# Attention output packed into 128 rows before the output projection, with a larger exponential ring and a new tile table

## The chip, the core and the metric

The kernel runs on one core of a Trainium2 chip. Its time is device microseconds of one execution. The engines are PE (TensorE, the matmuls), ACT (ScalarE), DVE (VectorE), POOL (GpSimd) and SP (SyncE, which here only issues DMAs).

## What is computed

One layer with attention and a feed-forward part side by side, on x of 2048 rows and 512 columns in bf16. There are 32 query heads of 16 columns; all share one key head and one value head.

```python
xn = layernorm(x)                                   # 2048 x 512
q  = (xn @ wq), 32 heads of 16;  k = xn @ wk;  v = xn @ wv     # k, v: 2048 x 16
o  = softmax(q @ k.T / 4) @ v                       # per head, over all 2048 keys
A  = concat(o) @ wo                                 # 2048 x 512
Bf = gelu(xn @ w1 + b1) @ w2 + b2                   # hidden width 1792
out = x + A + Bf
```

## The kernel before

**Stages.** A prologue loads x and the weights, normalises, transposes xn into xnT and makes keys, values and the first queries. Then the attention runs over 4 blocks (tb) of 512 query rows. A block has 8 groups (g) of 4 heads; group number gg = 8 tb + g counts 32 of them. A group has 64 score tiles, one for each head j of the group and each of 16 key tiles; a tile is 128 keys by 512 queries, one PSUM bank. All 2048 tiles are taken three at a time in 683 visits (u). PSUM has two sets of three banks for scores, so visit u+2 can be computed once visit u has been read.

**A visit.** `scores` (matmuls at L845, in four row tiles of 32) fills the three banks. `exp` (L864, ACT) makes the exponentials of two or three of them into the ring E of 20 slots. Where the string DTAB has a digit for the visit, the tile of that number goes to DVE instead: `p1` (L881) turns the score into an int16 that is read as bf16, and `close_batch` (L896) makes four more versions for up to three such tiles at a time; the five are summed with scaled copies of V. A dot in DTAB leaves all three tiles to ACT. `pv_mm` (L885) multiplies with V on PE in four column tiles of 32, one for each head of the group: one matmul for an ACT tile, five for a DVE tile. The result stands in PSUM bank 6 (pO), a head in each 32 rows: 16 rows of output, one row with the softmax sum.

**A group's end.** `o_evac` copies pO to Of (L909, DVE), an SP DMA collects the four rows of sums into den, DVE takes the reciprocal (L913), a DMA writes it to DRAM, four DMAs read it back spread over 32 rows each (rbc), and DVE multiplies Of by rbc into oT (L920). oT is a ring of 10 slots (NOT), each 128 x 512 with head j in rows 32j to 32j+15. The last group of all has its own short way (`o_norm_last`, L923 to L949), through PE transposes rather than DMAs.

**The out projection.** The weights wop are laid out like oT: 128 rows for each group, of which 4 x 16 hold rows of wo, the others zeros, and b2 in one of the rows that oT fills with ones. For each of 16 row tiles of 128, `out_tile` runs 14 steps of the feed-forward's second matmul (`y_mm`) and 8 steps on oT and wop (`wo_mm`), all into bank 7 (pM), each step as four column-tile matmuls by the helper `mm4` (L560). DVE adds x (L1010) and SP stores. Out tiles of block tb run in the beginning of block tb+1. For the last block, `y_tile` does the 14 steps and groups 0 to FIN_G - 1 ahead of time, the remaining groups follow at the end (L1133 on), and group 31 last.

**What sets the order.** The class `Prog` collects every operation with its reads, writes and an estimated duration, then `schedule` plays them through a model of the engines and fixes for each engine (and SP's DMAs) one order; `emit` writes these orders out with the semaphore waits that the dependences need. An argument `after` only shapes this order and makes no wait. A DMA counts in the model as 0.7 us of SP and 2.2 us to landing. Each DMA has a semaphore of its own stream; what waits for DMAs of several streams gets a wait instruction for each. Side work on PE (column-tile matmuls that are not pv) has a due time, ready time plus an allowance such as Y_ALLOW, and scores go first. Where PE would fall idle, the order gets fillers on zeros (L1152).

Of the kernel before, what the change touches and what calls it, by code (L numbers as in the profile page):

```python
# [10 lines left out]
P = 128  # L11
# [24 lines left out]
EV_ALLOW = -2.0  # L36
S_WAIT = 0.1
P_WAIT = 0.0
NE_ND_KB = (20, 8, 3)
LA = 34  # L40
LB = 105
LY = 9
LP = 121
LS = 107
FIN_G = 4
FIN_F = 0
LAL = 30.0
LCO = 0.0
PRO_FROM = 2.0
TBL = 1  # L50
DTAB = "....2.2020.202.2.2...22.202222..2022.20...2..2..20220.0.2222....2020.20.0202.0.002...2022.200...2.2000.0..220.2.2.0.202002020....002.2.22.0.2002.2...2.222002..02220.02...202.222202.02.2222....022222.202022..222...22200.00.0222.2022...2.20..22.2.2.20.20.....2020..2.22002020....20.22..020.222....0..22.0..2222.0...0220...20.00.0220.2200.22...22222.02.220.22220...2.22020.202202.022....2020.000.2200.2.0....202.2.2..220.0..2.0...0....2.0.2...22.00.....02220.2.222020.0....2.220.20...222222...2.22022.0022.2.2200....2222.22.202..2.22...2.220202.202.2202.0..2220.0000.222.220.....20.22.2200020..02....2..0...22...2.020.0....020202....2.02.20...2022.22.220.02022....22200222.2.2..202.0..."
Y_ALLOW = 8.0
H_ALLOW = 5.0
YT_ALLOW = (3,3,3,3)
WF_ALLOW = 1.5
# [370 lines left out]
def bass_parallel_sum__grouped_kv_mqa__dense_activation_gelu__prompt_kernel(  # L426
# [15 lines left out]
    S, D = xf.shape  # L442
    F = B_w1.shape[1]
    assert (S, D, F) == (2048, 512, 1792)
    H, Dh = 32, 16
# [3 lines left out]
    TBW = 512  # L449
    NTB = S // TBW  # L450
    HG = 4
    NGR = H // HG
    NE, ND, KB = NE_ND_KB
    NOT = 10
    NV = 1 + len(SPL_K)
    KZ = SPL_K.index(0)
    GAM = 128.0 / LN2 * 0.25
    bf, f32 = dt.bfloat16, dt.float32
    i16, i32 = dt.int16, dt.int32

    with ExitStack() as es:
        def sb(shape, dtype, name):
            return es.enter_context(nc.sbuf_tensor(name, shape, dtype))
# [6 lines left out]
        wvk = sb([P, DT, 2 * Dh], bf, "wvk")  # L470
        wkp = sb([P, DT, 4, 32], bf, "wkp")
        wqp = sb([P, DT, H, 32], bf, "wqp")
        wop = sb([P, NGR, D], bf, "wop")
        w1_sb = sb([P, DT, F], bf, "w1_sb")
        w2_sb = sb([P, FT, D], bf, "w2_sb")
        b1row = sb([FT, P], bf, "b1row")
# [3 lines left out]
        ones = sb([P, P], bf, "ones")  # L480
# [41 lines left out]
        rbc = sb([P, 2, TBW], f32, "rbc")  # L522
        rd_dram = nc.dram_tensor("rden_rows", [NTB * NGR, HG * TBW], f32).ap()
        oT = sb([P, NOT, TBW], bf, "oT")

        pAll = es.enter_context(nc.psum_tensor("pAll", [P, 8 * 512], f32))

        def bank(b, n=1):
            return pAll[:, b * 512:(b + n) * 512]
# [6 lines left out]
        def B(b):  # L536
            return ("bank", b)
# [19 lines left out]
        def mm4(o, l, rh, start, stop, r=(), w=(), allow=1.5, **ak):  # L557
            for j in range(4):
                c = slice(32 * j, 32 * j + 32)
                add("pe", lambda e, c=c, j=j: e.matmul(o[c, :], l[:, c], rh, start=start, stop=stop,  # L560
                                                       tile_position=(0, 32 * j)),
                    r, [(k, j) for k in w] + [k for k in w if k != B(7)], occ=0.216, lat=0.23, allow=allow, kind="side", tag=(None, j), **ak)
# [3 lines left out]
        def dma(eng, o, i, stream, r=(), w=(), lat=2.2, allow=1.0, **kw):  # L566
            return add(eng, lambda e: e.dma_start(o, i), r, w, dma=stream, occ=0.7, lat=lat, allow=allow, **kw)  # L567

        x_view = xf.rearrange("(t p) d -> p t d", p=P)
        for i in range(8):  # L570
            dma("sp", x_sb[:, 2 * i:2 * i + 2, :], x_view[:, 2 * i:2 * i + 2, :], f"d_x{i}",
                w=[("x", 2 * i), ("x", 2 * i + 1)], lat=2.3 + 0.5 * i, due=0.0)
# [8 lines left out]
        def setup(fn, r=(), w=(), occ=0.25, due=0.0, **kw):  # L581
            return add("pool", fn, r, w, occ=occ, lat=0.15, due=due, **kw)
# [17 lines left out]
              r=["wk_s", "wkp"], w=["wkp"], occ=0.45, due=2.0)  # L600
# [6 lines left out]
              r=["mrow"], w=["isc"], due=10.0)  # L607
        setup(lambda e: e.memset(crow[0:1, :], 1.13 * GAM * GAM), w=["crow"], due=10.0)
        setup(lambda e: e.memset(V1[:, :, :, Dh:32], 0.0), w=["V1"], occ=1.4, due=11.0)
        for v, c in enumerate((1.0,) + SPL_C):  # L610
# [3 lines left out]
              r=["mask4", "sel8"], w=["sel8"], due=12.0)  # L614
# [155 lines left out]
        for _, _, kind, a in sorted(steps, key=lambda s: s[:2]):  # L770
# [14 lines left out]
            r=[("std", LN_B[-1][0])] + ([("KT", ti) for ti in range(NT)] if TBL else []), w=["dum"], n=1600, due=1.0)  # L785
        dve(lambda e: e.tensor_reduce(kmx[:], kmax[:], AX.X, ALU.max), r=[("kmax", 0), ("kmax", NVA)], w=["kmx"], n=40, due=0.0)
        add("pe", lambda e: e.transpose(bank(3)[0:1, 0:P], kmx[:], ident_f[:]), r=["kmx", "ident_f"], w=[B(3)], occ=0.12, lat=0.22,
            due=0.0)
# [3 lines left out]
            r=["mrow"], w=[B(3), "ibi"], n=40, due=0.0)  # L792
        q_first_m(0, 7)
        dve(lambda e: e.tensor_copy(R2[:], bank(3)[:, 256:257]), w=[B(3), "R2"], n=40)
        for va, vb_ in ((0, NVA), (NVA, NT)):
# [3 lines left out]
                due=22.0)  # L799
            dve(lambda e, va=va, vb_=vb_: e.tensor_copy(V1[:, 0, va:vb_, 0:Dh], Vf[:, va:vb_, :]), r=["V1", ("Vf", va)], w=[("V", 0, va)],  # L800
                n=(vb_ - va) * Dh, due=22.1)
        for v, c in enumerate(SPL_C):
            setup(lambda e, v=v, c=c: e.tensor_scalar(V1[:, 1 + v, :, 0:Dh], Vf[:], c, None, ALU.mult),  # L803
                  r=["V1", ("Vf", 0), ("Vf", NVA)], w=[("V", 1 + v, 0), ("V", 1 + v, NVA)], occ=0.45, due=20.0)

        setup(lambda e: e.tensor_copy(wqp[:, :, 4:H, 0:Dh], wq_s[:, :, 64:D].rearrange("p k (h n) -> p k h n", n=Dh)),  # L806
              r=[("u", i) for i in range(8, 12)] + ["wqp"], w=["wqp"], occ=2.7, due=19.0, after=[pr.writer["ibi"]])
        setup(lambda e: e.tensor_scalar(sel8R[:], sel8[:], R2[:, 0:1], None, ALU.mult),
              r=["sel8", "R2"], w=["sel8R"], occ=0.5, due=22.0)
        late = [pr.writer["ibi"]]  # L810
        setup(lambda e: e.memset(wop[:], 0.0), w=["wop"], occ=3.0, due=24.0, after=late)
        setup(lambda e: e.tensor_copy(selL[:], ident[:, 16:113:32]), r=["ident"], w=["selL"], due=24.0, after=late)
        for j in range(HG):
            dma("sp", wop[32 * j:32 * j + Dh, :, :],
                bass.AP(A_wo.tensor, A_wo.offset + j * Dh * D, [[D, Dh], [HG * Dh * D, NGR], [1, D]]),
                f"d_wo{j}", w=["wop"])
        dma("sp", wop[16:17, 0, :], B_b2.rearrange("(o n) -> o n", o=1), "d_b2", w=["wop"])

        TPG = HG * NT
        NTILE = NTB * NGR * TPG  # L820
# [84 lines left out]
        onorm = {}  # L905

        def o_evac(gg):
            i = gg % 2
            dve(lambda e: e.tensor_copy(Of[:, i, :], pO), w=["O", ("Of", i)], allow=0.0)  # L909
            row = Of[16:17, i, :]  # L910
            dma("sp", den[:, i, :], bass.AP(row.tensor, row.offset, [[32 * row.ap[0][0], HG], [1, TBW]]),
                f"d_den{i}", r=[("Of", i)], w=[("den", i)])
            dve(lambda e: e.reciprocal(den[:, i, :], den[:, i, :]), r=[("den", i)], w=[("den", i)], n=120)  # L913
            dma("sp", rd_dram[gg:gg + 1, :], den[:, i, :], f"d_rd{i}", r=[("den", i)], w=[("rd", i)])
            for j in range(HG):
                src = rd_dram[gg:gg + 1, j * TBW:(j + 1) * TBW]
                dma("sp", rbc[32 * j:32 * j + 32, i, :], bass.AP(src.tensor, src.offset, [[0, 32], [1, TBW]]),
                    f"d_rb{i}{j}", r=[("rd", i)], w=[("rbc", i, j)])
            tb, g = divmod(gg, NGR)
            onorm[gg] = dve(lambda e: e.tensor_tensor(oT[:, gg % NOT, :], Of[:, i, :], rbc[:, i, :], ALU.mult),  # L920
                            r=[("Of", i)] + [("rbc", i, j) for j in range(HG)], w=[("oT", gg % NOT)], allow=3.0)

        def o_norm_last(gg):  # L923
            tb, g = divmod(gg, NGR)
# [68 lines left out]
                mm4(bank(bk), ub[:, ft, i * P:(i + 1) * P], w2_sb[:, ft, :], start and ft == fts[0], stop and ft == fts[-1],  # L993
                   r=[("u", ft), "w2"], w=[B(bk)], allow=al)

        def wo_mm(tb, i, gs, start=False, stop=True, bk=7, al=1.5):
            for n, g in enumerate(gs):
                assert tb * NGR + g in onorm
                mm4(bank(bk), oT[:, (tb * NGR + g) % NOT, i * P:(i + 1) * P], wop[:, g, :], start and n == 0,
                   stop and n == len(gs) - 1, r=[("oT", (tb * NGR + g) % NOT), "wop"], w=[B(bk)], allow=al)  # L1000

        def store(tb, i):
            ti = tb * 4 + i
# [1 line left out]

        def out_tile(tb, i):
            y_mm(tb, i, al=Y_ALLOW)
            wo_mm(tb, i, range(NGR), al=Y_ALLOW)
            ti = tb * 4 + i
            dve(lambda e: e.tensor_tensor(x_sb[:, ti, :], pM, x_sb[:, ti, :], ALU.add), w=[("x", ti)] + M4, allow=EV_ALLOW)  # L1010
            store(tb, i)
# [3 lines left out]
        def y_tile(tb, i):  # L1015
            ti = tb * 4 + i
            y_mm(tb, i, al=YT_ALLOW[i])
            wo_mm(tb, i, range(FIN_G), stop=i < 3, al=YT_ALLOW[i])
            if i < 3:
                dve(lambda e: e.tensor_tensor(xpy[:, i, :], pM, x_sb[:, ti, :], ALU.add), r=[("x", ti)],  # L1020
                    w=M4 + [("x", 2 * i), ("x", 2 * i + 1)], allow=EV_ALLOW)
            else:
                mm4(pM, ident, x_sb[:, ti, :], False, False, r=["ident", ("x", ti)], w=[B(7)], allow=YT_ALLOW[i])
# [57 lines left out]
        par, cgn = [0, 0], [0] * HG  # L1081
        if DTAB:
            for u, c in enumerate(DTAB):
                if c != ".":
# [21 lines left out]
        for u in range(NU):  # L1106
# [4 lines left out]
            for t in ts:  # L1111
                gg, kt, j = tile_of(t)
# [18 lines left out]
        tb = NTB - 1  # L1131
        FB = (2, 3, 4, 7)
        for i in range(4):  # L1133
            wo_mm(tb, i, range(FIN_G, NGR - 1), start=i < 3, stop=False, bk=FB[i], al=WF_ALLOW)
        for i in range(4):
            mm4(bank(FB[i]), oT[:, (NTB * NGR - 1) % NOT, i * P:(i + 1) * P], wop[:, NGR - 1, :], False, True,
               r=[("oT", (NTB * NGR - 1) % NOT) if i < 2 else ("oTl", 1), "wop"], w=[B(FB[i])], due=0.0)
        for i in (0, 1, 3, 2):
            ti = tb * 4 + i
            w = [(B(FB[i]), j) for j in range(4)] + ([B(FB[i])] if i < 3 else []) + [("x", ti)]  # L1140
            if i < 3:
                dve(lambda e, i=i, ti=ti: e.tensor_tensor(x_sb[:, ti, :], bank(FB[i]), xpy[:, i, :], ALU.add),
                    r=[("x", 2 * i), ("x", 2 * i + 1)], w=w)
# [7 lines left out]
        if FILL_GAP:  # L1151
            pr.filler = lambda e, j, o: e.matmul((pO if o else pM)[32 * j:32 * j + 32, :], zeros[:, 0:32], xnT[:, 0, 0:TBW],  # L1152
                                                 start=not o, stop=not o, skip_group_check=True,
# [37 lines left out]
```

## Time and profile before

| | |
|---|---|
| Median of 3 runs | 811.87 us (810.36 to 814.0) |
| The profiled execution | 811.03 us, span in the profile 809.2 us |
| Granted TensorE clock, mean | 0.987 |
| Busy: PE, ACT, DVE, POOL | 782.9, 785.3, 739.7, 23.7 us |
| First exponential starts, last one ends | 30.3 us, 799.5 us |
| Exponentials (L864) | 683, busy 748.2 us |
| Out-projection matmuls (wop with oT) | 512, in four bursts from 236.8 us on |
| DMA issues on SP | 301, 130.9 us |

Times in the profile are microseconds unless ns is written. A group line gives line, engine, operation, tiles as out<-in with their shapes, the count, then busy time and mean ns of one, then the idle time of the engine just before them and what ended it. "PEld" is the weight load of a matmul. The chain of waits goes back from the last instruction to what released it, step by step. In the view by stages, each engine has its busy time and the number of its instructions in the stretch, then the granted clock, the DMA share and GB/s.

### The profile page before, as it was taken

The page shows a single profiled execution, that of the slowest core. Times are in us where ns is not written, and L with a number is a line of the kernel's source. Part 1 is how long each engine was busy: PE and PEld are TensorE (multiplying, and loading weights), DVE is VectorE, ACT ScalarE, POOL GpSimd, SP SyncE. Part 2 cuts the span into 40 slices and gives each one's busy share as a digit, 9 for nine tenths or more (in the row PEclk, how much of TensorE's full clock was granted, in tenths as well). Part 3 has the DMA queues.
Part 4 walks back from the last instruction along what each step waited for, and adds up shares of the span by engine and source line. Part 5 has one row for each costly group of instructions (what it writes and reads, how often), then busy time and mean ns, then how long its engine had stood idle before and what let it go on. Part 6 is the DMA issues. An engine that isn't in the chain of part 4 may idle for free.

```text
span 809.2 us, 21055 instructions
## 1 busy us (share of the span) xinstructions
PE 782.9 (97%) x9082; PEld 245.4 (30%) x9082; DVE 739.7 (91%) x1403; ACT 785.3 (97%) x734; POOL 23.7 (3%) x79
## 2 busy tenths in 40 slices
PE   6799999999999999999999999999999999999998
PEld 4322322222323333333232333223232232233223
DVE  7499999999999978999999978799998897999985
ACT  4899999999999999999999999999999999999995
POOL 6500000000000000000000000000000000000000
PEclk7799999999999999999999999999999999999999
DMA  9000000000000000000000000000000000000001
GB/s 307 15 23 15 17 15 15 2 16 15 15 15 22 22 22 10 15 16 15 16 3 22 22 21 22 15 10 8 16 15 16 22 22 22 9 15 16 9 9 41
DMA packets 23975, 19.08 MB, mean 24 GB/s; under 512 B 12369, under 2 KB 19402, under 8 KB 23882
## 3 DMA queue, kind: packets, MB, share of 16 engines
q1 hardware_dynamic: 22298, 17.17, 7.5%
q8 instruction: 72, 1.18, 0.6%
q10 hardware_dynamic: 1584, 0.56, 0.3%
q14 instruction: 21, 0.17, 0.1%
HBM read 14.98 MB, written 2.35 MB: 21 GB/s over the span
## 4 chain that ended last, share of the span: by engine, by line
ACT 81%; PE 17%; DMA 1%; POOL 1%; issue 0%; DVE 0%; ACTq 0%; POOLq 0%
ACT E L864 77%; PE pAll L885 7%; PE pAll L845 5%; PE pAll L560 4%; ACT ub L987 3%; DMA ub<-in_A_wq_dram 1%; PE pAll L554 1%; ACT ub L684 0%; ACT xnT L702 0%; POOL V L803 0%; PE pAll L697 0%; POOL wqp L806 0%; ACT KT L716 0%; PE pAll L1152 0%; ACTq L567 0%
## 5 line engine op out<-in xcount | busy, mean ns | idle before, releaser
L864 ACT ACTIVATE E<-pAll 128x1024 bf16<-128x1024 f32 (+1 forms) x683 | 748.2, 1358 | 2.7 <-PE pAll L845 2.3
L885 PE MATMUL pAll<-Dt,V 128*32 128x512 bf16 x2070 | 362.7, 383 | 0.3 <-DVE Dt L896 0.2
L881 DVE TENSOR_SCALAR Dt<-pAll 128x512 int16<-128x512 f32 x414 | 278.4, 683 | 33.9 <-PE pAll L845 33.0
L885 PE MATMUL pAll<-E,V 128*32 128x512 bf16 x1634 | 297.1, 389 | 1.1 <-DVE Of L909 0.9
L896 DVE TENSOR_SCALAR Dt<-Dt 128x1536 int16<-128x1536 int16 (+2 forms) x584 | 283.1, 529 | 1.0
L845 PE MATMUL pAll<-QT,KT 32*128 32x512 bf16 x2048 | 268.5, 386 | 11.6 <-ACT E L864 4.2
L845 PEld LDWEIGHTS pAll<-QT,KT 32*128 32x128 bf16 x2048 | 67.8, 91 | 289.8 <-ACT E L864 246.5
L885 PEld LDWEIGHTS pAll<-Dt,V 128*32 128x32 bf16 x2070 | 99.1, 94 | 103.3 <-issue 50.8
L560 PE MATMUL pAll<-w_sb,ub 128*32 128x512 bf16 x896 | 115.3, 382 | 0.0
L560 PE MATMUL pAll<-xnT,w_sb 128*32 128x512 bf16 x896 | 109.5, 382 | 0.2
L885 PEld LDWEIGHTS pAll<-E,V 128*32 128x32 bf16 x1634 | 70.3, 93 | 80.8 <-issue 64.8
L560 PE MATMUL pAll<-wop,oT 128*32 128x512 bf16 x512 | 87.8, 381 | 0.0
L973 DVE TENSOR_SCALAR hb<-pAll,b1T 128x512 bf16<-128x512 f32 x56 | 41.6, 742 | 1.7 <-PE pAll L560 1.5
L560 PE MATMUL pAll<-xnT,wqp 128*32 128x512 bf16 x496 | 39.6, 391 | 0.8 <-DVE QT L739 0.4
L560 PEld LDWEIGHTS pAll<-xnT,w_sb 128*32 128x32 bf16 x896 | 29.5, 95 | 21.1 <-issue 7.5
L560 PEld LDWEIGHTS pAll<-w_sb,ub 128*32 128x32 bf16 x896 | 30.8, 95 | 13.2 <-issue 5.9
L987 ACT ACTIVATE ub<-ub 128x1536 bf16<-128x1536 bf16 (+1 forms) x20 | 32.3, 1617 | 0.0
L739 DVE CAST QT<-pAll 128x512 bf16<-128x512 f32 x32 | 21.9, 684 | 10.8 <-PE pAll L560 9.3
L1152 PE MATMUL pAll<-xnT,zeros 128*32 128x512 bf16 x300 | 31.0, 383 | 0.0
L560 PEld LDWEIGHTS pAll<-wop,oT 128*32 128x32 bf16 x512 | 24.5, 95 | 6.7 <-issue 1.5
L909 DVE COPY Of<-pAll 128x512 f32<-128x512 f32 x31 | 21.2, 682 | 0.5 <-PE pAll L885 0.2
L920 DVE TENSOR_TENSOR oT<-Of,rbc 128x512 bf16<-128x512 f32 x31 | 21.1, 682 | 0.0
(113 smaller groups left out, 262.4 us busy)
## 6 DMA issues: line engine op xcount, KB each, us to landing
rbc<-rden_rows SPq DMA_DIRECT2D x124, 64.0 KB, 2.0
w_sb<-in_B_w_dram SPq DMA_DIRECT2D x2, 1792.0 KB, 12.9
x_sb<-in_A_x_dram SPq DMA_DIRECT2D x8, 256.0 KB, 6.6
out_dram<-x_sb SPq DMA_DIRECT2D x16, 128.0 KB, 1.7
QT<-mT SPq DMA_DIRECT2D x60, 2.0 KB
ub<-in_A_wq_dram ACTq DMA_DIRECT2D x1, 512.0 KB, 7.4
wop<-in_A_wo_dram SPq DMA_DIRECT2D x4, 128.0 KB, 2.8
den<-Of SPq DMA_DIRECT2D x31, 8.0 KB
```

Of the source, the lines that this page charges most:

```text
L560: add("pe", lambda e, c=c, j=j: e.matmul(o[c, :], l[:, c], rh, start=start, stop=stop, tile_position=(0, 32 * j)), r, [(k, j) for k in w] ...
L739: dve(lambda e: e.tensor_copy(QT[:, hq, :], bank(bk)), w=[B(bk)] + [(B(bk), j) for j in range(4)] + [("QT", hq)] + [("QTm", hq, j) for j i ...
L845: ins = e.matmul(o, l, rh, start=True, stop=True, tile_position=(q0, 0))
L864: exps.append(act(lambda e: e.activation(E[:, s0:s0 + na, :], bank(b0, na).rearrange("p (a n) -> p a n", a=na), ACT.Exp, scale=LN2 / 128.0 ...
L881: dve(lambda e: e.tensor_scalar(Dt[:, KZ, s, :], bank(bk), float(127 * 128) + SPL_D, SPL_MIN, ALU.add, ALU.max), w=[B(bk), ("D", s, KZ)], ...
L885: add("pe", lambda e, a, b: e.matmul(pO[32 * j:32 * j + 32, :], V1[:, v, kt, :], rhs, start=a, stop=b, tile_position=(0, 32 * j)), r=r + [ ...
L896: dve(lambda e, k=k: e.tensor_scalar(Dt[:, k, s0:s0 + n, :], Dt[:, KZ, s0:s0 + n, :], float(SPL_K[k]), None, ALU.add), r=[("D", s0 + i, KZ ...
L909: dve(lambda e: e.tensor_copy(Of[:, i, :], pO), w=["O", ("Of", i)], allow=0.0)
L920: onorm[gg] = dve(lambda e: e.tensor_tensor(oT[:, gg % NOT, :], Of[:, i, :], rbc[:, i, :], ALU.mult), r=[("Of", i)] + [("rbc", i, j) for j ...
L973: dve(lambda e: e.tensor_scalar(hb[:, ft % 6, :], pM, b1T[:, ft:ft + 1], None, ALU.add), r=["b1T"], w=M4 + [("h", ft % 6)], allow=ev)
L987: act(lambda e: e.activation(uu, uu, ACT.Tanh, scale=GELU_K), r=uk, w=uk, n=c, allow=al - 0.5, kind="tanh")
L1152: pr.filler = lambda e, j, o: e.matmul((pO if o else pM)[32 * j:32 * j + 32, :], zeros[:, 0:32], xnT[:, 0, 0:TBW], start=not o, stop=not o ...
```

## The change

- **Packing.** When a group's oT is done, four DMAs on SP (one for each head, 16 rows of 1 KB) copy its 4 x 16 useful rows into a new ring oTp of 5 slots; an even group fills rows 0 to 63, the odd one after it rows 64 to 127. A slot thus holds 8 heads in 128 rows. oT keeps 3 slots.
- **Weights.** wop becomes wo as it is, 4 tiles of 128 rows, loaded in one DMA with no memset before it. The last group keeps the old layout with weights of its own, wol (a memset and four DMAs). b2 stands in the first row of b2row, the rest zeros.
- **Out projection.** `wo_mm` takes pairs of groups: 4 steps of all 128 rows in place of 8, and `b2_mm` adds a step with ones and b2row. In the last block, `y_tile` takes pairs 0 and 1 and the bias, the end takes pairs 2 and 3 (of pair 3 only group 30; a POOL memset clears the other half of its slot), and group 31 comes last with wol.
- **Ring and table.** E gets 24 slots in place of 20. DTAB is replaced: 416 digits in place of 414, and 212 of 683 entries differ.

```diff
-NE_ND_KB = (20, 8, 3)
+NE_ND_KB = (24, 8, 3)
...
-FIN_G = 4
+FIN_G = 2
...
-DTAB = "....2.2020.202.2.2...
+DTAB = "....2..020..02..22...
...
-    NOT = 10
+    NOT, NPR = 3, 5
...
-        wop = sb([P, NGR, D], bf, "wop")
+        wop = sb([P, NGR // 2, D], bf, "wop")
+        wol = sb([P, D], bf, "wol")
+        b2row = sb([P, D], bf, "b2row")
...
+        oTp = sb([P, NPR, TBW], bf, "oTp")
...
-        setup(lambda e: e.memset(wop[:], 0.0), w=["wop"], occ=3.0, due=24.0, after=late)
+        setup(lambda e: e.memset(wol[:], 0.0), w=["wol"], occ=0.4, due=24.0, after=late)
...
+        dma("sp", wop[:], A_wo.rearrange("(g p) n -> p g n", p=P), "d_wo", w=["wop"], after=late)
         for j in range(HG):
-            dma("sp", wop[32 * j:32 * j + Dh, :, :],
-                bass.AP(A_wo.tensor, A_wo.offset + j * Dh * D, [[D, Dh], [HG * Dh * D, NGR], [1, D]]),
-                f"d_wo{j}", w=["wop"])
-        dma("sp", wop[16:17, 0, :], B_b2.rearrange("(o n) -> o n", o=1), "d_b2", w=["wop"])
+            dma("sp", wol[32 * j:32 * j + Dh, :], A_wo[(H - HG + j) * Dh:(H - HG + j + 1) * Dh, :], f"d_wl{j}", w=["wol"])
+        setup(lambda e: e.memset(b2row[:], 0.0), w=["b2row"], occ=0.4, due=24.0, after=late)
+        dma("sp", b2row[0:1, :], B_b2.rearrange("(o n) -> o n", o=1), "d_b2", w=["b2row"])
...
+            pp, h = divmod(gg, 2)
+            if gg == NTB * NGR - 2:
+                setup(lambda e: e.memset(oTp[64:P, pp % NPR, :], 0.0), w=[("oTp", pp % NPR, 1, j) for j in range(HG)], occ=0.4)
+            for j in range(HG):
+                r0 = 64 * h + Dh * j
+                dma("sp", oTp[r0:r0 + Dh, pp % NPR, :], oT[32 * j:32 * j + Dh, gg % NOT, :], f"d_op{gg % NOT}{j}",
+                    r=[("oT", gg % NOT)], w=[("oTp", pp % NPR, h, j)])
...
-        def wo_mm(tb, i, gs, start=False, stop=True, bk=7, al=1.5):
-            for n, g in enumerate(gs):
-                assert tb * NGR + g in onorm
-                mm4(bank(bk), oT[:, (tb * NGR + g) % NOT, i * P:(i + 1) * P], wop[:, g, :], start and n == 0,
-                   stop and n == len(gs) - 1, r=[("oT", (tb * NGR + g) % NOT), "wop"], w=[B(bk)], allow=al)
+        def wo_mm(tb, i, ps, start=False, bk=7, al=1.5):
+            for n, p in enumerate(ps):
+                pp = tb * NGR // 2 + p
+                hs = [h for h in range(2) if 2 * pp + h < NTB * NGR - 1]
+                assert all(2 * pp + h in onorm for h in hs)
+                mm4(bank(bk), oTp[:, pp % NPR, i * P:(i + 1) * P], wop[:, p, :], start and n == 0, False,
+                   r=[("oTp", pp % NPR, h, j) for h in range(2) for j in range(HG)] + ["wop"], w=[B(bk)], allow=al)
+
+        def b2_mm(bk=7, stop=True, al=1.5):
+            mm4(bank(bk), ones, b2row[:], False, stop, r=["ones", "b2row"], w=[B(bk)], allow=al)
...
-            wo_mm(tb, i, range(NGR), al=Y_ALLOW)
+            wo_mm(tb, i, range(NGR // 2), al=Y_ALLOW)
+            b2_mm(al=Y_ALLOW)
...
-            wo_mm(tb, i, range(FIN_G), stop=i < 3, al=YT_ALLOW[i])
+            wo_mm(tb, i, range(FIN_G), al=YT_ALLOW[i])
+            b2_mm(stop=i < 3, al=YT_ALLOW[i])
...
-            wo_mm(tb, i, range(FIN_G, NGR - 1), start=i < 3, stop=False, bk=FB[i], al=WF_ALLOW)
+            wo_mm(tb, i, range(FIN_G, NGR // 2), start=i < 3, bk=FB[i], al=WF_ALLOW)
...
-            mm4(bank(FB[i]), oT[:, (NTB * NGR - 1) % NOT, i * P:(i + 1) * P], wop[:, NGR - 1, :], False, True,
-               r=[("oT", (NTB * NGR - 1) % NOT) if i < 2 else ("oTl", 1), "wop"], w=[B(FB[i])], due=0.0)
+            mm4(bank(FB[i]), oT[:, (NTB * NGR - 1) % NOT, i * P:(i + 1) * P], wol[:, :], False, True,
+               r=[("oT", (NTB * NGR - 1) % NOT) if i < 2 else ("oTl", 1), "wol"], w=[B(FB[i])], due=0.0)
```

More of the change, by code (lines that the diff above doesn't have):

```diff
@@ L50 @@
 TBL = 1
-DTAB = "....2.2020.202.2.2...22.202222..2022.20...2..2..20220.0.2222....2020.20.0202.0.002...2022.200...2.2000.0..220.2.2.0.202002020....002.2.22.0.2002.2...2.222002..02220.02...202.222202.02.2222....022222.202022..222...22200.00.0222.2022...2.20..22.2.2.20.20.....2020..2.22002020....20.22..020.222....0..22.0..2222.0...0220...20.00.0220.2200.22...22222.02.220.22220...2.22020.202202.022....2020.000.2200.2.0....202.2.2..220.0..2.0...0....2.0.2...22.00.....02220.2.222020.0....2.220.20...222222...2.22022.0022.2.2200....2222.22.202..2.22...2.220202.202.2202.0..2220.0000.222.220.....20.22.2200020..02....2..0...22...2.020.0....020202....2.02.20...2022.22.220.02022....22200222.2.2..202.0..."
+DTAB = "....2..020..02..22...22.202220..20.00.0...220...222200..02200...2.02.2200.00220.02...20222.20...022.0000...2002.0.2.20000.000...2020.2220.0..20020....02.222.0022020..2...202.202202.02.222.....02.222.2022.000.22...20220.00.0222.2022...2220.02..2.2.0022......022...20.202002.2......02.0.000222.00.0..22.0..222..200000......2200.02202.000.22....2220.02.220.22220...22.2020.202202.022....2022.20022.0000.0....20222.220020....220..22..0...0.0..20.00.....022.20..20222.002....20220.20...22022.....0.20202.0.222.220....2220222.00222.2.22...222.0022.00222.0.20...2.020000.222.222.......202.0200.0...02......0...022...22.200....002.202...02.02.20...2022.22..20.020222...22202200..220.2000...."
 Y_ALLOW = 8.0
```

## The prediction

> **What bounds the kernel now.** I read first the page's busy shares and its chain, then the groups with shapes kept apart, then busy time by stage, the waits of PE and ACT, and the timeline of the last 10 us.
>
> ```profile
> PE 782.9 (97%) x9082; PEld 245.4 (30%) x9082; DVE 739.7 (91%) x1403; ACT 785.3 (97%) x734; POOL 23.7 (3%) x79
> ACT 81%; PE 17%; DMA 1%; POOL 1%; issue 0%; DVE 0%; ACTq 0%; POOLq 0%
> L864 ACT ACTIVATE E<-pAll 128x1024 bf16<-128x1024 f32 x415 | 428.1, 1194 | 0.9 <-PE pAll L845 0.8
> L864 ACT ACTIVATE E<-pAll 128x1536 bf16<-128x1536 f32 x268 | 401.0, 1613 | 1.8 <-PE pAll L845 1.5
> ```
>
> Three engines look full, but the chain that ends last is ACT for 81% of the span: the exponentials (L864), one per visit of three score tiles. A visit with one tile sent to DVE (a digit in DTAB) covers two banks, the others three. ACT is idle before them for 2.7 us in all. PE's 97% says less: four column tiles overlap, so a matmul record of 380 ns stands for about 55 ns of issue, and 300 of its matmuls are fillers (L1152, on zeros).
>
> Next, busy time in seven stages from the first exponential to the last, and the out-projection's own matmuls in the same stages:
>
> ```profile
> core 0: us, PE busy (x) PEld busy (x) DVE busy (x) ACT busy (x) POOL busy (x), PEclk, DMA share, GB/s
> 30.30:223.00 192.70, 186.94 (x2045) 54.80 (x2042) 182.82 (x347) 192.38 (x177) 7.78 (x6) 0.98 0.06 15
> 223.00:304.00 81.00, 80.50 (x1026) 24.60 (x1023) 72.49 (x137) 80.77 (x78) 0.00 (x0) 1.00 0.08 20
> 304.00:415.00 111.00, 108.41 (x1179) 33.33 (x1175) 108.78 (x205) 110.03 (x101) 0.00 (x0) 1.00 0.05 13
> ...
> 223.00:304.00 81.00, 24.18 (x128) 7.10 (x128) 0.00 (x0) 1.00 0.08 20
> 799.50:809.20 9.70, 5.14 (x73) 1.82 (x67) 0.00 (x0) 1.00 0.17 56
> ```
>
> The last two rows are for the matmuls on wop alone. Where the out tiles run (223 to 304, and again at 415 and 609) PE is the tight second engine (12.7 matmuls per us) and DVE has air (72.5 of 81); where they don't, DVE is nearly full (108.8 of 111). ACT is full in both.
>
> How much is ACT losing? Starts of successive exponentials, read singly off the timeline, are 0.904 us apart after two banks and 1.331 after three in over half of the visits. DTAB has 414 digits and 269 dots: 414 x 0.904 + 269 x 1.331 = 732.3; 16 long tanh at 1.36 and 4 short at 0.94 (the chain's steps for L987) add 25.5; together 757.8. From the first exponential (30.34) to the end of the last (799.54) are 769.2, so about 11 us of late scores are spread over 683 visits. They, the 9.7 us tail and ACT's own count are all that a change behind the softmax can reach.
>
> **What the skill says.** "ScalarE: Activation LUTs", What ACT_TABLE_LOAD costs, gives one element per cycle, 0.833 ns: 427 ns for 512 columns. The trace agrees: 1.331 - 0.904 = 0.427. "TensorEngine Tiling (Array Packing)", Key Properties, says that changing the tiling mode drains the TensorE; the trace agrees as far as it shows the 0.23 us that the weight load after a score visit loses to "issue" over and over. So time saved inside a visit's column work is real, but no visit goes away. "DMA: Bandwidth & Descriptors", Anatomy of one DMA, puts some 2 us fixed on a DMA; its fit is for another issue path, so I use this trace: rbc lands in 2.0 us.
>
> **The change, part by part.**
>
> *Out projection.* Before, 16 tiles x 8 groups x 4 column tiles = 512 matmuls (the page has x512). After: twelve tiles x 5 steps, four x 6 (the last block keeps group 31 apart, on wol), x 4 = 336. Gone are 176 matmuls, 44 fours. In the chain 16 matmuls took 1.05 us and 8 took 0.61, so a four adds 0.22: 9.7 us of PE, 2.6 at each of three block boundaries (12 fours) and 1.8 in the last block (8 fours, half of them in the tail). In the boundaries it lies beside ACT, which is full: worth part of the stalls only, between 0 and, generously, a third of the 11 us there and elsewhere; I take 0.7 gained.
>
> *Packing DMAs.* 31 groups x 4 on SP. SP's 301 issues took 131 us. The nearest rows are den<-Of (0.574 us) and QT<-mT (0.559), both from SBUF to SBUF: 124 x 0.56 = 69 us, SP then works 200 of 809. Behind each, in order, stand the next group's den DMA, stores and the QT<-mT of the next block. A group's oT is finished 13 to 23 us after its Of copy, the next Of copy comes about 23 us after the last, and a pack takes 2.2 us of issue: none is held up for long. Cost nothing while oT leads the next den; if it didn't, the next group's reciprocal slips by 2 us of a lead of many. From oT's end to the last landing: 4 x 0.56 + 2.0 = 4.3 us. In the quickest group the Of copy starts at 291.0 and its reciprocal at 294.3, so copy (0.68), issue and landing fit in 3.3: the other bound is 2.6 per single DMA, which puts the last landing at about 4.3 too.
>
> *Who waits for it.* PE, in an order written beforehand. Block 0: oT of group 7 ends at 236.57, so it lands near 240.9; the 32 wop matmuls of the first out tile ran from 236.75 to 244.56 and pairs 0 to 2 now go first. Block 1: 433.10 + 4.3 = 437.4 against an old end of 435.61. Block 2: 622.78 + 4.3 = 627.1 against 627.47. The order is planned with 0.7 us per issue and 2.2 to land, 5.0 in all, longer than my 4.3. So the usual case is no stall. Queued behind a wo matmul that does wait are scores, and behind those ACT, which has one visit, 0.9 to 1.3 us, in hand.
>
> *Semaphores.* The first use of a pair now waits on eight DMA streams where a DVE ticket served; about 16 x 8 wait instructions on PE. No row prices one. Zero if they run in the shadow of earlier matmuls; 0.44 us per pair if they don't (55 ns each, as one matmul, is my estimate: no row has it), 7 us at the outside, of which ACT's visit in hand hides most. I take +0.5. DVE's norm also waits for the pack of three groups before, some 60 us old: nothing.
>
> *DTAB.* 416 digits against 414: two tiles leave ACT, 2 x 0.427 = -0.85 us, on the path. They cost DVE 2 x (0.68 + 4 x 0.17) = 2.7 us and PE eight matmuls, 0.4 us. 212 of 683 entries differ; by sixteenths of the list the large shifts go to the stretches behind the second and third block boundary (24 to 28 and 27 to 30 digits), away from stretches without out tiles (27 to 25, 27 to 23). That is where PE got air. No gain is counted beyond the 0.7 above; a reshuffle can lose as much.
>
> *E ring.* 24 slots for 20. No exponential waits for a slot now (its waits name scores): 0.
>
> *Prologue.* wop's 3.5 us memset on POOL goes, two short ones come, later than POOL's links of the chain. The 512 KB of wop now carry no wait and follow w2 directly, some 1.7 us at the first slice's 307 GB/s, behind x, w1 and w2 in the same queue: nothing waits for them. The four old wop issues (1.5 us each) no longer straddle QT<-mT at 41 us, which has time: 0. The one POOL memset of half a pack slot meets an idle POOL: 0.
>
> *Tail.* From the last exponential (799.54) to 809.2, PE alternates the last norm with 73 wop matmuls; the last link is 39 matmuls to 806.16, then ACT's copy and the store. 16 fewer in the tail and fewer left over from before give 0.9; the final matmuls need oT's second half (804.13) in any case, so 1.2 at most. Against it: group 30's oT ended at 797.38, packed by 801.7; its 16 matmuls (0.9) then end near 802.6, before the last norm's 804.1. I take -1.0; late by over 1.5 us, the pack sets the end and the gain is gone.
>
> Sum: -0.85 - 1.0 - 0.7 + 0.5 = -2.05. The profiled execution took 811.03 (span 809.2), the median 811.87, 0.84 above, inside the spread of the three (810.36 to 814.0). The difference put on the median: 809.8.
>
> **Rivals.** Differences under 0.5% (4.1 us, so 807.8 to 815.9) are about what a measurement of this kernel can tell from no change.
>
> *The forecast: hidden anyway* (0.47). PE's relief lies beside a full ACT. Own range 807.8 to 813.5.
>
> *Slower: the first use of each pair stops PE* (0.30). Sixteen places where eight waits and a landing stand in PE's fixed order, in front of scores. It decides once the stop exceeds ACT's visit in hand, that is, once landing is over 1 us later than planned or the waits aren't shadowed. With 0.6 us lost on ACT at each of 16, 9.6, less the 1.85 of table and tail: 819.6. For it: PE has little air at the boundaries, and DVE, nearly full elsewhere, can run behind the plan and delay oT. Against: today not one wop matmul waits for a norm from L920, and the plan's latency is the longer one. A table that starves ACT would look the same in time, but with waits for DVE.
>
> *Faster: the air reaches ACT* (0.23). If PE's relief and tiles moved to it close 4 of the 11 us: -0.85 - 1.2 - 4 = -6.05, 805.8. For it: PE is 17% of the chain, mostly in the boundaries and the last 60 us. Against: ACT idles only 2.7 us visibly, and most of the 11 is in crumbs of under 0.1 us per visit.
>
> *It does not do what it says*: then wop matmuls would not fall to 256 plus 64 on b2row and 16 on wol; the time would stay at 811.
>
> The range leaves out the far end of each outer rival: 804 to 820.
>
> **What would show it.** Right: 416 and 267 exponentials by form, ACT idle before them near 3 us, 336 out-projection matmuls, more filler (over 300), SP near 200 us, the last link shorter than 39 matmuls. Wrong, slower: weight loads of L560 waiting for DMA oTp, or exponentials for scores by over 10 us in all; wrong, faster: the stretch from first to last exponential below 764 us.

## The result and the profile after

| | before | after |
|---|---|---|
| Median of 4 runs | 812.78 us (810.36 to 814.0) | 806.38 us (805.92 to 807.92) |
| The profiled execution | 811.03 us, span 809.2 | 807.92 us, span 806.2 |
| First exponential starts | 30.34 us | 30.28 us |
| First exponential to the end of the last | 769.2 us | 767.1 us |
| Late scores in it (counted as in the prediction) | 11.4 us | 10.2 us |
| End of the last exponential to the end | 9.65 us | 8.76 us |

The ratio is 0.9928 (95% interval 0.9899 to 0.9957): 0.7% faster, some 6 us by the medians. A second set of runs of the same kernel, with more runs of before, gave 0.9941 (0.9925 to 0.9957), some 5 us. The two profiled executions are only 3.1 us apart, and the table above accounts for all of that: 2.1 between the first and the last exponential, 0.9 in the tail. Late scores are, as in the prediction, what that stretch is longer than the sum of its exponentials (0.904 or 1.331 us each) and its tanh pieces; they are counted in this way for every run below.

From the page of the kernel after: busy shares, the chain by engine, and groups (line engine op, tiles and shapes, count, then busy time and mean ns, then idle time before).

```profile
PE 773.6 (96%) x8944; PEld 242.4 (30%) x8946; DVE 740.6 (92%) x1409; ACT 784.1 (97%) x734; POOL 21.8 (3%) x81
...
ACT 89%; PE 8%; DMA 1%; POOL 1%; DVE 0%; issue 0%; ACTq 0%; DVEq 0%
...
L563 PE MATMUL pAll<-wop,oTp 128*32 128x512 bf16 x256 | 54.3, 381 | 0.0
L1169 PE MATMUL pAll<-xnT,zeros 128*32 128x512 bf16 x332 | 35.5, 383 | 0.0
...
oTp<-oT SPq DMA_DIRECT2D x124, 16.0 KB, 1.8
```

ACT is the chain for 89% of the span, where it was 81%; PE's share fell from 17 to 8%. The out projection is down to 256 matmuls here, with 64 for the bias and 16 for the last group, 336 as the diff says. Fillers on zeros rose from 300 to 332: a part of PE's air is filled with nothing. That air isn't where the out tiles run: from 304 to 415 us there are 88 fillers where there were 28.

The exponentials by shape, from the groups with shapes kept apart, and three of the stages, whose bounds are those of before (busy time and count of PE, PEld, DVE, ACT, POOL):

```profile
L867 ACT ACTIVATE E<-pAll 128x1024 bf16<-128x1024 f32 x417 | 424.6, 1202 | 0.9 <-PE pAll L848 0.8
L867 ACT ACTIVATE E<-pAll 128x1536 bf16<-128x1536 f32 x266 | 394.4, 1614 | 0.7 <-PE pAll L848 0.6
```

```profile
223.00:304.00 81.00, 80.19 (x1030) 24.10 (x1024) 72.86 (x141) 81.00 (x78) 0.00 (x0) 1.00 0.08 22
304.00:415.00 111.00, 107.84 (x1189) 33.03 (x1185) 107.32 (x196) 111.00 (x102) 0.00 (x0) 1.00 0.07 17
415.00:491.00 76.00, 75.33 (x945) 22.57 (x948) 69.29 (x134) 75.98 (x75) 0.00 (x0) 1.00 0.09 23
```

Two visits more have two banks (417 for 415; the last visit of all has two tiles and no digit). PE is as dense in the boundaries as it was: 1030 matmuls from 223 to 304 where there were 1026, although the out projection lost 48 there (80 for 128). The plan filled the air at once. DVE gained work in the stretches where it had air (134 instructions for 127 from 415 to 491) and lost it in one of those where it was nearly full (196 for 205 from 304 to 415), but not in the next (213 for 207 from 491 to 609).

The tail, as the end of the chain of waits of the kernel after (start, length, what):

```profile
799.66 0.44 PE pAll L954 x2
800.10 0.33 PE pAll L563 x4
800.43 0.37 PE pAll L954 x2
800.80 0.65 PE pAll L563 x8
801.45 0.02 issue
801.47 1.29 DVE x_sb L1159 x2
```

The block of 39 matmuls ahead of the last copy is gone; 8 stand in its place, and the end is set by DVE, which adds the residual to three row tiles (1.9 us).

### The profile page after: what moved, and what is told of

Same layout as the page of the kernel before. It is cut to its first block, busy times and chain, and to the rows that moved or that the text cites. A ratio compares the mean times of both kernels' runs of the same rounds, so it can differ in the third digit from the quotient of the medians.

```text
span 806.2 us, 20980 instructions
## 1 busy us (share of the span) xinstructions
PE 773.6 (96%) x8944; PEld 242.4 (30%) x8946; DVE 740.6 (92%) x1409; ACT 784.1 (97%) x734; POOL 21.8 (3%) x81
## 4 chain that ended last, share of the span: by engine, by line
ACT 89%; PE 8%; DMA 1%; POOL 1%; DVE 0%; issue 0%; ACTq 0%; DVEq 0%
ACT E L867 84%; ACT ub L997 3%; PE pAll L888 3%; PE pAll L848 2%; PE pAll L563 2%; DMA ub<-in_A_wq_dram 1%; PE pAll L557 1%; ACT ub L687 1%; ACT xnT L705 0%; POOL V L806 0%; POOL wqp L809 0%; ACT KT L719 0%; PE pAll L700 0%; DVE x_sb L1159 0%; ACTq L570 0%
## 5 line engine op out<-in xcount | busy, mean ns | idle before, releaser
L888 PE MATMUL pAll<-E,V 128*32 128x512 bf16 x1632 | 300.2, 388 | 0.4 <-DVE Of L912 0.4
L563 PE MATMUL pAll<-w_sb,ub 128*32 128x512 bf16 x896 | 118.1, 382 | 0.2 <-DVE hb L983 0.2
L563 PE MATMUL pAll<-xnT,w_sb 128*32 128x512 bf16 x896 | 113.2, 382 | 0.3
L563 PE MATMUL pAll<-wop,oTp 128*32 128x512 bf16 x256 | 54.3, 381 | 0.0
L563 PE MATMUL pAll<-xnT,wqp 128*32 128x512 bf16 x496 | 41.6, 396 | 0.8 <-POOL wqp L809 0.6
L563 PEld LDWEIGHTS pAll<-xnT,w_sb 128*32 128x32 bf16 x896 | 31.2, 95 | 20.5 <-issue 5.7
L1169 PE MATMUL pAll<-xnT,zeros 128*32 128x512 bf16 x332 | 35.5, 383 | 0.0
L994 DVE TENSOR_TENSOR ub<-hb 128x1536 bf16<-128x1536 bf16 (+1 forms) x20 | 18.0, 899 | 0.2
```

Of the source, the lines that this page charges most:

```text
L888: add("pe", lambda e, a, b: e.matmul(pO[32 * j:32 * j + 32, :], V1[:, v, kt, :], rhs, start=a, stop=b, tile_position=(0, 32 * j)), r=r + [ ...
```

## The experiments

Theories. A: the prediction's sum of small terms. B: the new table is the source. C: PE's relief is the source. D, formed after the first four runs: what decides is how well the table and the plan made from it fit each other, so that no part has a worth of its own. In three runs (those whose heading says that a plan is kept) the order of every engine is that of the kernel they start from (ACT, DVE, POOL and SP run the same instructions in the same order); in the others the edit has it planned anew. Ratios are to the kernel before, run on the same chip; each diff is against the kernel named in its heading.

**The change again.**

> The changed kernel once more, as the measure for the parts. Theory A (a sum of small things: two tiles off ACT, a shorter tail, fewer late scores) and the rivals all expect the ratio to before near 0.993, that is 5 to 7 us; from the two profiles, 3.0 us of span were explained: 0.9 by table counts, 1.2 by late scores, 0.9 by the tail. If this run's ratio is near 0.996, those three terms are the whole; if it stays at 0.993, some 3 us lie outside what the first pair of profiles shows.

Measured: 0.9941 (0.9925 to 0.9957), median 807.14. Its profiled execution (807.18 us, span 805.4) has the same stretch of exponentials, 767.2 us, and a first exponential at 29.57. So 3 us of the gain are located, and what is beyond lies in the scatter of executions: the start of the first exponential lies between 28.9 and 30.3 in three profiles of one and the same plan (these two, and the one-semaphore run below). Where the rest of it comes from stays open.

**The new table alone** (against before).

```diff
-DTAB = "....2.2020.202.2.2...
+DTAB = "....2..020..02..22...
```

> Only the new DTAB, on the old packing, E of 20 slots. Theory A: 2 x 0.427 us less on ACT, and more PE work just where the out tiles still take 8 steps, so between 1 us faster and 3 us slower. Rival B (the table is the source): at least half of the gain, 3 us or more faster. Rival C (PE's relief is the source, and the table only fills it): slower by 2 to 6 us, with exponentials waiting for scores behind the second and third block boundary.

Measured: 830.17 us, 1.0224 (1.0204 to 1.0243): 18 us slower. B falls, and the loss is far beyond what A and C allowed. Late scores are 18.4 us for 11.4, but most of the loss is the tail, 24.6 us for 9.65. The end of its chain:

```profile
805.25 0.70 DVE ub L989
...
810.26 4.39 PE pAll L560 x76
...
815.42 4.17 PE pAll L560 x72
...
820.37 5.25 PE pAll L560 x92
```

The last GELU piece is done at 805.9, after the last exponential, and three of the last block's row tiles are computed whole behind it, 4 to 5 us each. Feed-forward matmuls on w_sb (both layers), in the stretch up to the last exponential and after it, show this in one view for before, after and this run, in this order:

```profile
30.00:799.50 769.50, 223.97 (x1790) 60.17 (x1790) 0.99 0.06 16
799.50:809.20 9.70, 0.89 (x3) 0.18 (x2) 1.00 0.17 56
```

```profile
30.00:797.40 767.40, 231.36 (x1792) 63.53 (x1792) 0.99 0.07 18
797.40:806.20 8.80, 0.00 (x0) 0.00 (x0) 1.00 0.20 65
```

```profile
30.00:803.80 773.80, 207.23 (x1616) 56.51 (x1616) 0.99 0.06 16
803.80:828.40 24.60, 10.22 (x176) 4.43 (x176) 1.00 0.07 23
```

Before leaves 3 of 1792 over, after none, the new table on the old packing 176.

**The packing alone**, and **with the ring**, both on the old table (against after).

```diff
-NE_ND_KB = (24, 8, 3)
+NE_ND_KB = (20, 8, 3)      # the packing alone; 24 in the other run
-DTAB = "....2..020..02..22...
+DTAB = "....2.2020.202.2.2...
```

> Only the packing: old DTAB, E of 20 slots. Theory A: tail 0.9 us shorter, late scores up to 1.2 us fewer, so 1 to 2 us faster. Rival B: within 1 us of before. Rival C: 4 us or more faster.

> Packing and the ring of 24 slots, old DTAB. Theory A: as with the packing alone (no exponential waits for a slot), 1 to 2 us faster than before. Rival B: within 1 us of before. Rival C: 4 us or more faster. If the ring matters by itself, this is faster than the packing alone by over 1 us.

Measured: 819.13 us, 1.0084 (1.0066 to 1.0102), and 818.26 us, 1.0075 (1.0056 to 1.0094). A, B and C had none of them expected a loss of this size; with these runs D was formed. PE has 176 matmuls fewer and yet late scores are 19.3 and 16.1 us, the tail 11.7 in both, with 58 feed-forward matmuls left over in the first. The same table gives another order once the work changes, and a worse one.

**A part of PE's relief alone, the plan of before kept** (against before). It leaves the shares of the narrowed groups out of the output.

```diff
+ light = g in ((1, 3, 5) if tb < NTB - 1 else (1, 5))
- mm4(bank(bk), oT[...], wop[:, g, :], ...)
+ mm4(bank(bk)[:, 0:1] if light else bank(bk), oT[...], wop[:, g, 0:1] if light else wop[:, g, :], ...)
```

> The kernel before with its plan untouched, but 3 of the 8 out-projection steps of each row tile in blocks 0 to 2 and 2 of 7 in the last are one column wide, so PE is relieved of 176 matmuls of 512 columns, as by the packing; those groups' shares are left out of the output. No table, ring, DMA or order changes. Theory A (PE's relief lies beside a full ACT, worth late scores and tail): 1 to 3 us faster than before. Theory C (the relief by itself is the gain): 5 us or more faster. Theory D (what counts is whether table and plan fit each other, found only by searching): within 3 us, as the plan is the old fitted one.

Measured: 0.9997 (0.9982 to 1.0012), 810.21 us. ACT's waits for scores, before and in this run, then the busy shares of this run:

```profile
ACT E L864 <- PE pAll L845: 2.3, 4, 0.9
```

```profile
ACT E L864 <- PE pAll L845: 2.3, 5, 0.8
PE 780.7 (97%) x9082; PEld 245.6 (30%) x9082; DVE 739.1 (91%) x1403; ACT 785.2 (97%) x734; POOL 24.2 (3%) x79
```

Late scores are 11.5 us for 11.4 and the stretch of exponentials 769.3 for 769.2. Only the tail is shorter, 9.1 for 9.65. But the relief is smaller than it was meant to be. The record of a narrow matmul is 169 ns for 381, and in most visits the other column tiles still run full ones beside it: of the 89 visits that have narrow matmuls, only 10 have their column work shortened by over 0.1 us. PE's busy time falls by 2.2 us, where the change takes 9.3 off it (782.9 to 773.6). So single column tiles made lighter were worth nothing that shows; what 9.7 us taken off whole steps would be worth in this order was not tested, so this run settles neither A's term nor C.

**Matmuls added back, the plan of after kept** (against after).

```diff
+ for j, op in enumerate(pr.ops[-4:]):   # the four column tiles of a step
...
+     def fn(e, f=op.fn, c=c, j=j):
+         for _ in range(pad):  # 3 at each bias step, 1 in the last block, 1 with its last pairs
+             e.matmul(o[c, :], zeros[:, c], xnT[:, 0, 0:TBW], start=False, stop=False, tile_position=(0, 32 * j))
+         return f(e)
```

> The changed kernel with its plan untouched, but each bias step issues 3 more matmuls on zeros (1 in the last block, and 1 more with the last pairs): PE does 512 out-projection matmuls again. Theory A: gives back 1 to 3 us. Theory C: gives back all of the 5 us and more. Theory D, that the new table was made for the relieved PE and needs its room: 5 to 15 us slower than the change, with a longer tail, as with the new table alone.

Measured: 821.71 us, 1.013 (1.0109 to 1.0151): 14.6 us over the 807.14 of the change, 14.0 over the 807.72 of the next run, which has the same plan and ran on the same chip. D's range held, its place only partly: the loss is in late scores, 23.8 us for 10.2, at the boundaries of all blocks (visits 168 to 250, 360 to 420, 532 to 590), while the tail is 9.2. ACT's waits and the busy shares, then the end of the chain:

```profile
ACT E L867 <- PE pAll L848: 9.5, 23, 0.7
PE 789.8 (96%) x9122; PEld 251.8 (31%) x9122; DVE 742.4 (91%) x1409; ACT 788.5 (96%) x734; POOL 22.6 (3%) x81
```

```profile
808.09 0.61 DVE oT L923
808.72 0.52 SPq L570
...
810.55 2.58 DMA oTp<-oT
813.17 0.44 PE pAll L954 x2
```

The 176 matmuls hold PE for longer than the 9.7 us at which the prediction priced as many. The planner spreads the four column tiles of a step over its order, and here three added matmuls and the bias matmul stand one behind another on one column tile, with the next scores behind them. One of 21 such places, from the timeline of PE:

```profile
252.41 0.81 PE L1024 MATMUL pAll<-xnT,zeros 128*32 128x512 bf16 x3
253.06 0.38 PE L563 MATMUL pAll<-b2row,ones 128*32 128x512 bf16 x1
253.37 0.39 PE L848 MATMUL pAll<-QT,KT 32*128 32x512 bf16 x3
```

From the start of each added matmul to that of PE's next one are 18.2 us in all 176, and PE's busy time rises by 16.2 (773.6 to 789.8). Most of that came out as time. What the 176 would cost if they were spread as the old steps were, and whether the plan of before would take the same blocks any better, was not tried. So this run and the one before it can't be set against each other as one relief given and taken back. This run also shows the tail's danger: oT of group 30 comes late, and its pack, landed 4.4 us after oT's end, holds the end of the chain.

**One semaphore for a group's four packs, the plan of after kept** (against after).

```diff
- f"d_op{gg % NOT}{j}"
+ f"d_op{gg % NOT}"
```

> The changed kernel with its plan untouched, but the four packing DMAs of a group count on one semaphore, so the first use of a pair waits for two streams rather than eight and the norm for one rather than four: some 95 wait instructions fewer on PE. The prediction's price was +0.5 us for these waits (0 to 7): here at most 0.5 us faster than the change. The rival that the waits stop PE: 3 us or more faster.

Measured: 0.9956 (0.9939 to 0.9972), 807.72 us, against 0.9941 (0.9925 to 0.9957) for the change: no gain, and exponentials and tail take 767.5 and 8.6 us for 767.1 and 8.8. The wait instructions cost nothing that this can tell; the two intervals still leave room for the half us of the prediction.

**A ring of 20 slots in the change** (against after).

```diff
-NE_ND_KB = (24, 8, 3)
+NE_ND_KB = (20, 8, 3)
```

> The change with a ring of 20 slots. Theory A: within 0.5 us of the change, since no exponential is seen waiting for a slot. If the ring gives PE needed freedom to let pv work lie: 2 to 5 us slower, with the first difference of the traces near an exponential that waits for pv.

Measured: 0.9972 (0.996 to 0.9983), 808.56 us, some 1 to 2.5 us slower than the change. Up to visit 624 late scores agree with those of the change to 0.1 us, and ACT and DVE have the same order. There ACT waits once for a slot (for pv, which reads it):

```profile
ACT E L867 <- PE pAll L848: 1.4, 3, 0.8
...
ACT E L867 <- PE pAll L888: 1.1, 1, 1.1
```

The second row is not there in the change. The stretch of exponentials is 768.3 us for 767.2, and late scores are 11.4, as before the change.

**No fitted table on either side** (against before; the other two have the packing as well). An empty DTAB lets the kernel's own rule choose; it chooses the same 418 tiles with and without packing.

```diff
-DTAB = "....2.2020.202.2.2...
+DTAB = ""
```

> The kernel before with an empty DTAB: the kernel's own simple rule picks the tiles for DVE, the same ones whether there is packing or not, so a table that was fitted to neither kernel. Theory D (time is held by how well table and plan fit): 5 to 20 us slower than before. Theory A says nothing on it.

> Packing, ring of 20, the same rule-made table as in the run beside it. Compared with that run this is the packing with no fitted table on either side. Theory C (relief is a gain by itself): 5 us or more faster than that run. Theory A: 1 to 3 us faster. Theory D: either sign, within 6 us.

> Packing, ring of 24, the same rule-made table: the ring alone with an unfitted table. From the ring with the old table (0.9 us of the median) and with the new one (1 to 2.5 us): 1 to 3 us faster than with 20 slots. If no exponential waits for pv in the other run, equal within 1 us.

Measured: before 840.51 us, 1.0354 (1.0329 to 1.0379); packing with 20 slots 829.3, 1.0222 (1.0195 to 1.025); packing with 24 slots 836.46, 1.031 (1.0287 to 1.0332). Here the packing gives 11 us (tail 15.3 for 29.0, 86 feed-forward matmuls left over for 224), as C alone had expected (5 us or more), and the larger ring takes 7 back (tail 21.9), the opposite of what it does with the new table. The ring's expectation missed in sign and D's "within 6 us" was too narrow. But C had also expected 4 us or more from the packing with the old table, where it lost 7. With 20 slots throughout, the packing is worth 7 us lost with the old table, 11 gained with none, and some 20 gained with the new one (0.9972 against 1.0224): no single worth fits it.

**Eight digits turned** (against before). Visits 69, 140, 223, 304, 393, 460, 540, 621: "2" becomes "0" in the table of before.

> The kernel before with 8 of the 414 digits turned from 2 to 0, some 80 visits apart: another tile of the same visit goes to DVE, the work of every engine stays the same in total. Theory D: the plan is made anew from the first of them on, and the time moves by 2 to 8 us, more likely up. If the table's exact entries don't matter: within 1 us.

Measured: 837.11 us, 1.0312 (1.0291 to 1.0332): 25.6 us slower, three times the top of what D expected. DVE, ACT and PE have the same work in total, fillers apart. Late scores are 18.3 us for 11.4 and the tail is 31.0: 233 feed-forward matmuls come behind the last exponential.

```profile
30.00:803.30 773.30, 200.01 (x1561) 54.23 (x1561) 0.99 0.06 16
803.30:834.30 31.00, 15.57 (x233) 7.00 (x231) 1.00 0.06 19
```

This is one set of eight digits; others weren't tried.

The ring of 24 slots without the packing wasn't tried either. What the packing frees in SBUF is what the ring takes: oT 7 KB less a partition, wop 4 less, oTp 5 more, wol and b2row 1 each, the ring 4 more.

## Why the prediction was right or wrong

The direction held, and 806.38 lies in 804 to 820, a range wide enough for both outer rivals. The likeliest case was too small: 809.8, and its own range ended at 807.8. The outcome is that of the faster rival in size (805.8), but not by its mechanism: late scores fell by 1.2 us, not by 4, and the stretch of exponentials is 767.1 us, not below 764. That the time came out in the range is in part luck, as two of the terms were wrong and 2 to 3 us of the gain have no cause that a trace shows.

- **Table, -0.85.** Right: two exponentials changed shape, and with 20 slots the stretch of exponentials is 768.3 for 769.2, 0.9 less with nothing else gone.
- **Late scores from PE's relief, -0.7.** Wrong term. With the packing and the new table but 20 slots, late scores are 11.4 us, as before. The 1.2 us came with the ring.
- **Ring, 0.** Wrong. No exponential waited for a slot before; that was no proof for a plan made anew. In the new plan 20 slots cost one wait of 1.1 us. The step that failed is reading a row that is missing in one plan as one that will be missing in the next.
- **Semaphores, +0.5.** Nothing was seen of it, as at the low bound of 0; the runs don't exclude half a us.
- **Tail, -1.0.** Right: -0.9, with group 30's packs landed in time.
- **Packs.** The sum to landing, 4 x 0.56 + 2.0 = 4.3 us, counts the last issue twice, since the profile's 2.0 runs from an issue's start. From oT's end to the last of the four landings the median of 31 groups is 3.7 us (3.7 to 5.6). SP is busy 219.6 us, for about 200. No wop matmul waits for an oTp landing, so the slower rival did not come about; but the last four wop matmuls of a block's first row tile started only 0.7, 1.5 and 0.4 us after the block's last pack had landed, so little was to spare.
- **Prologue.** The first exponential starts 0.1 us earlier, which is inside the scatter of one plan (28.9 to 30.3). The one DMA for wop held SP for 7.8 us, which the prediction didn't foresee; nothing waited for it.

With these values the sum is -0.9 - 1.1 - 0.9 - 0.1 = -3.0, which is what the spans of the profiled executions differ by. The medians say 5 to 6, and the intervals reach down to 3.5; of what lies beyond the 3.0 no trace shows a cause.

The larger miss isn't in a term. The prediction took the table as two tiles and a reshuffle that "can lose as much" as 0.7 us. Shown by undoing each: the table without the packing costs 18 us, the packing without the table 7, and eight digits of equal work 25.6. The packing and the table are each a loss by themselves beside the old partner. What the change compares is one pair of plan and table that fit each other with another such pair. (How the two tables were found is not on record; that they fit is read from how much worse their neighbours are.)

Where the runs with unfitted pairs lose shows two parts. Feed-forward matmuls don't get done before the last exponential (58 to 233 where they were counted, while the two fitted kernels leave 3 and 0), and so the tail is 12 to 31 us. With the old out projection this is most of the loss; with the packing, late scores are more of it (16 to 27 us). That the fitted pairs avoid both is shown; why one order packs the work and the other doesn't is not, since each plan differs from the place of its first difference on.

## What to carry to other kernels

Where a planner turns a table into a fixed order, don't price the parts of a change against the old order. The packing was worth 7 us lost, 11 gained or 20 gained with three tables; the table has to be fitted again before a part is judged. If the order is held to isolate the work of one engine, first read on the profile how much of its time the edit moved: 176 matmuls made narrow took 2.2 us off PE's busy time, and 176 added ones put 16.2 on it. Look also at how much side work is left behind the last instruction of the bounding engine, beside the late starts on it: in these runs the two together are where every bad plan lost.

## What was not expected of the hardware

- Wait instructions on PE for six more DMA streams at the first use of a pair were not to be seen in the time: 0.9956 with two streams, 0.9941 with eight, the intervals overlapping.
- What a matmul costs depends on the column tiles beside it. In the run with matmuls added back, four of 512 columns in a row on one column tile held PE for 0.96 us (252.41 to the scores at 253.37); 16 of the same shape over four column tiles took 1.19 us (241.58 to the scores at 242.77).
- A DMA of 16 rows of 1 KB from SBUF to SBUF takes SP 0.59 us to issue (median of 124) and lands 1.8 us after its issue starts. Of the 3.7 us that a group's four take, some 2.4 are issue.
